# Own buffers for the last rows' queries, a third key load buffer, and six bias groups ahead of the first step

## The chip, the cores and the metric

The kernel runs on one NeuronCore of a Trainium2 chip. The metric is the device time of one execution in microseconds (us). The core has five engines that run side by side, each with its instructions in a fixed order: PE (matrix products and transposes, which it does as matrix products; PEld is its weight load), DVE (vector), ACT (activation functions, copies), POOL (general vector work) and SP, which here only issues DMA transfers. An engine that reaches an instruction whose input is not there yet stands still, and all that is behind it on that engine stands too.

## What is computed

The reference chains three layers on 2 x 576 tokens of width 512: attention with a learnt bias, a token and channel mixer, and a layer of eight experts with one expert chosen for each token. The change touches the first alone:

```python
scores = scale * np.matmul(q, k.transpose(0, 1, 3, 2))          # 2 batches, 8 heads, 576 x 576, head size 64
x = (psi_rel / psi_i)[..., None]                                # log1p(|i - j|) / log1p(max(i, 1))
h = np.maximum(x @ w1 + b1, 0.0)                                # 32 hidden values for each (i, j)
scores = scores + (h @ w2).transpose(2, 0, 1)[None]             # one bias for each head, same in both batches
attn = softmax(scores)                                          # row maximum taken away, exp, divided by the sum
out = np.matmul(attn, v)
```

## The kernel before

**Steps.** Attention runs in 40 steps, each for one pair of heads of one batch and one tile of query rows. The 576 rows are four tiles of 128 and a tail of 64. The tail comes first: steps 0 to 7 (`it == NIT`), eight pairs, four for each batch. Steps 8 to 15 are the first full tile, and so on. In a step `scores` multiplies on PE and calls `softmax_tile`, which adds the bias and finds the row maximum on DVE (L337) and takes exp on ACT (L340); `normalize` (DVE, POOL), `last_T` and `prob_T` (transposes), `values` and `out_T` follow in the same step or the next two.

**Keys.** During the tail every step also transposes the keys of the pair two steps on (`key_T`: PE, copies on ACT and DVE) and splits them in two parts (`key_split`: DVE, L272). Keys are loaded for two pairs at a time by `load_k` (five transfers); `load_k(0)` and `load_k(2)` come in the start, `load_k(4)` too, `load_k(6)` after step 1, and all share two buffers `kn`. `load_v` is ten transfers for one batch.

**Queries.** For tail steps, `tail_split` (POOL) and `tail_T` put the transposed queries into `qts`, two buffers for two steps each. For full steps `query_T`, `query_split` and `query_rest` prepare two steps at a time and write them into the same `qts` with four transfers from SP (`qt<-qs`, 128 KB each, L328). `load_q` reads them from memory into two buffers `qn` (128 KB).

**Bias.** The bias is made in 36 groups of 16 rows. I count them from 0: groups 0 to 3 are the tail's rows, 4 to 11 the first full tile's. For a group, `bias_hidden` makes four 128 x 576 tiles (L487 on ACT, L490 on DVE and POOL), `bias_mm` multiplies them on PE (16 matmuls, L500), ACT copies the result to `ev` (L503), and SP sends `ev` to the rows of the tile `bias` (L509 for the tail, L511 else, 288 KB a group). `ev` has two buffers, so the copy of group n + 2 waits until the transfer of group n has landed. The softmax of a tile needs all its groups. Groups 0 to 4 are made ahead of step 0; then each step makes one (`bias_mm`) and the hidden tiles of the next, so group 11 falls in step 6. Step 7 makes none, and step 8 begins with group 12.

**Order.** Nothing is scheduled by a tool: the lists in `ORDER` say in which order the parts of a step are written down, and each engine takes its share in that order. `start` is what comes ahead of step 0, `first` is for steps 0 to 2, `mixed` for 3 to 7, `bias` for later ones. `load_q` of a step is issued ahead of its list.

Of the kernel before, what the change touches and what calls it, by code (L numbers as in the profile page):

```python
# [9 lines left out]
F32 = mybir.dt.float32  # L10
F32R = mybir.dt.float32r
# [10 lines left out]
B, H, S, D = 2, 8, 576, 64  # L22
# [26 lines left out]
MROWS = E * CAP + 10 * 128  # L49

WARM = 3
AHEAD = 1
QRB = 2
TB = 2
QO = 3, 3, 3, 6

ORDER = {
    "start": "hidden0 const load_k2 tail_split0 hidden1 bias0 hidden2 bias1 key_T00 hidden3 zero key_T01 key_T11 key_T10 key_split0 tail_split1 bias2 hidden4 bias3 load_k4 hidden5 key_split1 tail_T bias4 load_v load_q".split(),
    "first": "scores0 hidden2 last_T prob_T0 values key_T0 normalize query_T tail_T query_split hidden1 hidden0 key_T1 bias_mm key_split out_T tail_split hidden3 query_rest".split(),
    "mixed": "hidden2 scores0 values tail_T query_T normalize hidden0 last_T prob_T0 key_T0 key_T1 query_split tail_split hidden1 key_split query_rest bias_mm out_T hidden3".split(),  # L60
    "bias": "query_T query_split hidden3 scores0 scores1 last_T values hidden0 query_rest hidden2 late bias_mm out_T mix prob_T0 prob_T1 hidden1 normalize".split(),
# [71 lines left out]
def attention(tc, nc, tok, mix, q, k, v, w1, b1, w2, c_L, c_id, ident, x, wt1, wt2, prefill):  # L133
# [4 lines left out]
    NP = H // 2  # L138
# [4 lines left out]
    tw_p = pool(tok, "tokw")  # L143
    with ExitStack() as ctx:
        cst = pool(ctx, "acst")
        bias_p = pool(ctx, "bias", 2)
        nat_p = pool(ctx, "nat")
# [62 lines left out]
        def load_k(i):  # L210

            b, pr = divmod(i, NP)
            n = nat_p.tile([128, 20, D], F32, name="kn", tag="kn", bufs=2)
            main, hs = n[:, 0:16].rearrange("p (n h) d -> p n h d", h=4), k[b, 2 * pr:2 * pr + 4]
            for j in range(NIT):
                nc.sync.dma_start(main[:, j], hs[:, 128 * j:128 * j + 128].rearrange("h p d -> p h d"))
            nc.sync.dma_start(n[0:64, 16:20], hs[:, 512:S].rearrange("h p d -> p h d"))
            for j in range(2):
                nat["k", i + j] = main[:, :, 2 * j:2 * j + 2], n[0:64, 16 + 2 * j:18 + 2 * j]
# [14 lines left out]
        def load_q(it, i):  # L234

            b, pr = divmod(i, NP)
            n = nat_p.tile([128, 4, D], F32, name="qn", tag="qn", bufs=2)
            if it == NIT:
                tv = q[b, :, 512:S].rearrange("(a e) p d -> e p a d", e=2)
                for e in range(2):  # L240
                    nc.sync.dma_start(n[64 * e:64 * e + 64], tv[e])
                for j in range(NP):
                    nat["q", it, i + j] = n[:, j]
            else:
                nc.sync.dma_start(n, q[b, 2 * pr:2 * pr + 4, 128 * it:128 * it + 128].rearrange("h p d -> p h d"))
                nat["q", it, i] = n
# [29 lines left out]
        QT = {}  # L276
        qts = [nat_p.tile([128, 2, 4, 128], F32R, name=f"qt{i}") for i in range(2)]

        def query_tile(s):
            return qts[s // 2 % 2][:, s % 2]  # L280

# [1 line left out]

        def query_zero():

            for qt in qts:
                nc.gpsimd.memset(qt[:, :, 0:2, 64:128].bitcast(F32), 0.0)
                nc.gpsimd.memset(qt[:, :, 2:4, 0:64].bitcast(F32), 0.0)

        def tail_split(it, i):  # L290
            n = nat.pop(("q", it, i))
# [5 lines left out]

        def tail_T(it, i):
            qs = nat.pop(("qs", it, i)).bitcast(F32).rearrange("p a d -> p (a d)")
            QT[it, i] = qt = query_tile(i)  # L300
            tp = alloc_ps()
            for a in range(2):
                nc.tensor.transpose(tp[:, 128 * a:128 * a + 128], qs[:, D * a:D * a + 128], ident)
            tv = tp[:, 0:256].rearrange("p (a i) -> p a i", a=2)
            scaled("qT0", qt[:, 0:2, 0:64], tv[:, :, 0:64])
            scaled("qT1", qt[:, 2:4, 64:128], tv[:, :, 64:128])
# [277 lines left out]
        steps = [(it, i) for it in its for i in range(B * NP)]  # L584
# [23 lines left out]
        def late_fetch(s):  # L608
# [4 lines left out]
        load_const()  # L613
        bias_setup()
        start = {
            "const": (bias_const,), "zero": (query_zero,), "load_k2": (load_k, 2), "load_k4": (load_k, 4), "load_v": (load_v, 0),
            "load_q": (load_q, *steps[NP]), "tail_T": (tail_T, *steps[0]),
        }
        for n in range(2):
# [11 lines left out]
        for s in range(N + 2):  # L631

            bias = gi < len(groups) and s < N and s >= B * NP * (its.index(groups[gi] // 8) - 1)
            at = lambda d, n=N: steps[s + d] if 0 <= s + d < n else None
            two = lambda d: (s + d) % 2 == 0 and s + d >= B * NP and at(d)
            hide = groups[gi + 1] if bias and gi + 1 < len(groups) else None
            todo = {
                "late": (late_step, (s,)), "mix": (mixes[s][0], mixes[s][1:]) if s in mixes else (None, None),
                "tail_split": (tail_split, at(2, B * NP)), "tail_T": (tail_T, at(1, B * NP)),
                "query_T": (query_T, two(QO[0])), "query_split": (query_split, two(QO[1])), "query_rest": (query_rest, two(QO[2])),  # L640
                "key_split": (key_split, at(2, B * NP)),
                "normalize": (normalize, at(0)), "last_T": (last_T, at(-1)),
                "values": (values, at(-2)), "out_T": (out_T, at(-2)),
# [2 lines left out]
            for j in range(4):  # L646
# [1 line left out]
                todo[f"key_T{j}"] = key_T, j < 2 and at(2, B * NP) and (*at(2), j)  # L648
                todo[f"scores{j}"] = scores, at(0) and (*at(0), j)
                todo[f"prob_T{j}"] = prob_T, at(-1) and (*at(-1), j)  # L650
            if two(QO[3]):
                load_q(*steps[s + QO[3]])
            for name in ORDER["edge" if bias and s % (B * NP) == B * NP - 1 else "first" if s < 3 else "mixed" if s < B * NP else "bias" if bias else "plain"]:
                f, a = todo[name]
                if a:
                    f(*(a[1:] if f in (key_split, key_T) else a))
            gi += bias
            late_fetch(s - 1)
            if s == 1:
                load_k(6)  # L660
            if s == 2:
                load_v(1)
            if s == 10:
# [639 lines left out]
class Experts:  # L1303
# [7 lines left out]
    AHEAD = [[f"big{4 * a + c}.0" for c in range(4)] for a in range(2)]  # L1311
# [451 lines left out]
```

## Time and profile before

| | |
|---|---|
| median of 3 runs | 584.0 us (583.43 to 585.43) |
| the profiled execution | 584.03 us, of it the span 582.3 us |
| busy share of the span | PE 94%, DVE 66%, ACT 57%, POOL 42% |
| attention's first 80 us | the tail's steps lie between about 21 and 64 us, step 8 begins at about 64 |

The span is what the profiler saw of the core; all times of rows are counted from its start. A line of a timeline has the start, the duration, the engine, the line of the code, the operation and its tiles, and in brackets how long the engine had been idle and what it waited for last. SPq is SP's queue: the time that the issue of a transfer took, not the transfer. Where a row joins several instructions, "x4" is their number and the duration that of all.

### The profile page before, as it was taken

The page shows a single profiled execution, that of the slowest core. Times are in us where ns is not written, and L with a number is a line of the kernel's source. Part 1 is how long each engine was busy: PE and PEld are TensorE (multiplying, and loading weights), DVE is VectorE, ACT ScalarE, POOL GpSimd, SP SyncE. Part 2 cuts the span into 40 slices and gives each one's busy share as a digit, 9 for nine tenths or more (in the row PEclk, how much of TensorE's full clock was granted, in tenths as well). Part 3 has the DMA queues.
Part 4 walks back from the last instruction along what each step waited for, and adds up shares of the span by engine and source line. Part 5 has one row for each costly group of instructions (what it writes and reads, how often), then busy time and mean ns, then how long its engine had stood idle before and what let it go on. Part 6 is the DMA issues. An engine that isn't in the chain of part 4 may idle for free.

```text
span 582.3 us, 11959 instructions
## 1 busy us (share of the span) xinstructions
PE 545.5 (94%) x4306; PEld 430.3 (74%) x4306; DVE 383.9 (66%) x896; ACT 329.5 (57%) x608; POOL 242.1 (42%) x230
## 2 busy tenths in 40 slices
PE   7689699999899999989999999999999999999992
PEld 3366477777677887869999877787778778787871
DVE  5789588889887675698888535714473235668650
ACT  4678589789898793344444223221423257777760
POOL 4666547476555360044444300310014234657541
PEclk8979889999999999999999999999999999999997
DMA  6997988698697351143443020081002985566950
GB/s 162 130 173 126 142 158 165 132 177 157 127 147 126 77 154 38 37 138 120 148 161 126 1 91 0 1 302 61 19 18 43 370 299 175 147 230 245 367 185 12
DMA packets 72110, 79.90 MB, mean 137 GB/s; under 512 B 36822, under 2 KB 51420, under 8 KB 72044
## 3 DMA queue, kind: packets, MB, share of 16 engines
q1 hardware_dynamic: 67276, 73.72, 50.7%
q0 software_dynamic: 2176, 5.26, 2.7%
q8 instruction: 36, 0.59, 0.5%
q10 hardware_dynamic: 2592, 0.09, 0.3%
q14 instruction: 30, 0.25, 0.2%
HBM read 72.08 MB, written 5.34 MB: 133 GB/s over the span
## 4 chain that ended last, share of the span: by engine, by line
PE 65%; DVE 12%; DMA 7%; issue 5%; ACT 5%; SPq 2%; POOL 2%; ACTq 0%; POOLq 0%; DVEq 0%
PE ph L748 20%; PE po L748 16%; DMA bias<-ev 6%; PE py L748 5%; PE ps L500 5%; PE tp L425 4%; PE ps L359 3%; PE tp L410 3%; DVE t L337 2%; ACT t L340 2%; PE tp L748 1%; DVE K L272 1%; DMA mt<-meta 1%; PE tp L1448 1%; DVE raw L732 1%
## 5 line engine op out<-in xcount | busy, mean ns | idle before, releaser
L490 POOL TENSOR_SCALAR hd<-tabs,sc,negb 128x576 f32<-128x576 f32 x32 | 76.4, 2389 | 4.7 <-PE ps L500 3.0
L340 ACT ACTIVATE t<-t,st 128x576 f32<-128x576 f32 x72 | 55.4, 770 | 28.8 <-DVE st L337 28.4
L748 PE MATMUL po<-cw,h 128*128 128x512 f32 x272 | 67.3, 395 | 0.0
L337 DVE CUSTOM_DVE_ANT_0 t<-ps,bias 128x576 f32<-128x576 f32 x72 | 52.3, 751 | 16.1 <-DMA bias<-ev 6.6
L359 PE MATMUL ps<-K,qt 128*128 128x288 f32 x320 | 54.0, 309 | 4.4 <-DVE qt L199 3.5
L748 PEld LDWEIGHTS po<-cw,h 128*128 128x128 f32 x272 | 49.8, 188 | 10.0 <-issue 0.4
L1411 DVE TENSOR_TENSOR big<-raw,big 128x1024 fp32r<-128x1024 f32 x30 | 42.3, 1433 | 22.4 <-ACT big L1410 22.4
L500 PE MATMUL ps<-hd,wblk 128*32 128x288 f32 x576 | 47.7, 440 | 7.5 <-DVE st L337 6.5
L359 PEld LDWEIGHTS ps<-K,qt 128*128 128x128 f32 x320 | 45.0, 192 | 6.7 <-DVE qt L199 2.3
L425 PE MATMUL tp<-pt,v 128*64 128x128 f32 (+1 forms) x800 | 49.2, 268 | 0.6 <-DVE K L272 0.6
L748 PE MATMUL py<-big,hT 128*128 128x512 f32 x184 | 47.8, 400 | 0.4 <-POOL big L1411 0.4
L1189 POOL DMA_INDIRECT meta<-tokid,posi x10 | 10.0, 996 | 90.7 <-DVE tokid L1186 54.7
L425 PEld LDWEIGHTS tp<-pt,v 128*64 128x64 f32 x800 | 40.1, 137 | 8.1 <-issue 5.1
L1410 ACT CAST big<-raw 128x1024 fp32r<-128x1024 f32 x44 | 44.2, 1055 | 2.8 <-DMA big<-in_moe_w_dram 1.0
L748 PE MATMUL ph<-big,xT 128*128 128x512 f32 x168 | 42.9, 403 | 0.0
L490 DVE TENSOR_SCALAR hd<-tabs,sc,negb 128x576 f32<-128x576 f32 x69 | 42.2, 640 | 1.0 <-PE ps L500 0.9
L748 PEld LDWEIGHTS py<-big,hT 128*128 128x128 f32 x184 | 33.8, 188 | 8.6 <-POOL big L1411 0.9
L740 POOL TENSOR_TENSOR big<-wf,big 128x512 fp32r<-128x512 f32 x12 | 18.8, 1564 | 50.3 <-ACT big L739 50.3
L487 ACT ACTIVATE hd<-tabs,b1c,sc 128x576 f32<-128x576 f32 x43 | 36.9, 866 | 3.8 <-DVE sc L458 3.7
L1411 POOL TENSOR_TENSOR big<-raw,big 128x1024 fp32r<-128x1024 f32 x10 | 27.5, 2747 | 24.9 <-ACT big L1410 24.3
L748 PEld LDWEIGHTS ph<-big,xT 128*128 128x128 f32 x168 | 30.6, 189 | 8.6 <-issue 1.6
L500 PEld LDWEIGHTS ps<-hd,wblk 128*32 128x32 f32 x576 | 17.2, 115 | 24.1 <-DVE st L337 7.9
(302 smaller groups left out, 1204.7 us busy)
## 6 DMA issues: line engine op xcount, KB each, us to landing
raw<-in_moe_w_dram SPq DMA_DIRECT2D x48, 512.0 KB
raw<-in_moe_w_ch_dram SPq DMA_DIRECT2D x24, 512.0 KB
bias<-ev SPq DMA_DIRECT2D x32, 288.0 KB
qt<-qs SPq DMA_DIRECT2D x64, 128.0 KB
lw<-in_moe_w_dram SPq DMA_DIRECT2D x16, 512.0 KB
big<-in_moe_w_dram SPq DMA_DIRECT2D x8, 512.0 KB
lw<-in_moe_w_dram SPq DMA_DIRECT2D x16, 256.0 KB
big<-in_moe_w_dram SPq DMA_DIRECT2D x16, 256.0 KB
```

What stands on the lines that cost most here:

```text
L337: nc.vector.tensor_tensor_reduce(t.rearrange("p (a j) -> p a j", a=2), ps[:, :, 0:HALF], bs.rearrange("p (a j) -> p a j", a=2), op0=ALU.ad ...
L340: nc.scalar.activation(t, t, AF.Exp, bias=st[:, j:j + 1], scale=-1.0, accum_out=st[:, 2 + j:3 + j])
L359: nc.tensor.matmul(ps[:, hf, 0:HALF], lhsT=qt[:, j], rhs=K[k][:, hf * HALF:(hf + 1) * HALF], start=j == pairs[0][0], stop=j == pairs[-1][0])
L410: nc.tensor.transpose(tp[:, 128 * j:128 * j + 128], tt[:, o:o + 128], ident)
L425: nc.tensor.matmul(po[64 * h:64 * h + 64, 0:rhs.shape[1]], lhsT=lhsT, rhs=rhs, start=j == 0, stop=j == 4)
L487: nc.scalar.activation(hd[:, qq], Lt[:, o:o + S], AF.Relu, bias=b1c, scale=sc[:, c])
L490: eng.tensor_scalar(hd[:, qq], Lt[:, o:o + S], sc[:, c], negb, ALU.mult, ALU.max)
L500: nc.tensor.matmul(ps[32 * qq:32 * qq + 32, hf, 0:HALF], lhsT=wblk, rhs=hd[:, qq, hf * HALF:(hf + 1) * HALF], start=True, stop=True)
L740: nc.gpsimd.tensor_tensor(lo, src, hi.bitcast(F32), ALU.subtract)
L748: nc.tensor.matmul(out, lhsT=lhs[a], rhs=rhs[b], start=first and i == 0, stop=last and i == 2)
L1410: nc.scalar.copy(hi, raw)
L1411: (nc.gpsimd if c == 3 and t else nc.vector).tensor_tensor(lo, raw, hi.bitcast(F32), ALU.subtract)
```

## The change

- The tail's queries get a tile of their own, `lastq`, with a place for each of two steps, in memory that `w2s` takes later; `query_zero` clears that in place of `qts`.
- `load_k(4)` goes into a third buffer, `kn2`, in memory that is used later for `wt1_s`. `load_k(6)` thereby takes the first buffer, and is moved from after step 1 to the start, behind `load_v` and `load_q`.
- `AHEAD` is 2: six groups of the bias come ahead of step 0, so hidden tiles of group 6 and the whole of group 5 stand in `start`, group 5 as its last entry. Each group after that is made one step sooner, group 11 in step 5; steps 6 and 7 make none.
- The queries of steps 8 and 9 are prepared in step 4 instead of step 5. All others stay.

```diff
-AHEAD = 1
+AHEAD = 2
-QO = 3, 3, 3, 6
+QO = 3
-    "start": "hidden0 const load_k2 tail_split0 hidden1 bias0 hidden2 bias1 key_T00 hidden3 zero key_T01 key_T11 key_T10 key_split0 tail_split1 bias2 hidden4 bias3 load_k4 hidden5 key_split1 tail_T bias4 load_v load_q".split(),
+    "start": "hidden0 const load_k2 tail_split0 hidden1 bias0 hidden2 bias1 key_T00 hidden3 zero key_T01 key_T11 key_T10 key_split0 tail_split1 bias2 hidden4 bias3 load_k4 hidden5 key_split1 tail_T bias4 load_v hidden6 load_q load_k6 bias5".split(),
...
-            n = nat_p.tile([128, 20, D], F32, name="kn", tag="kn", bufs=2)
+            if i == NP:
+                n = nat_p.tile([128, 20, D], F32, name="kn2", tag="ks")
+            else:
+                n = nat_p.tile([128, 20, D], F32, name="kn", tag="kn", bufs=2)
...
+        lastq = tw_p.tile([128, 2, 4, 128], F32R, name="lastq", tag="w2s")
...
-            for qt in qts:
-                nc.gpsimd.memset(qt[:, :, 0:2, 64:128].bitcast(F32), 0.0)
-                nc.gpsimd.memset(qt[:, :, 2:4, 0:64].bitcast(F32), 0.0)
+            for qt in (lastq[:, 0], lastq[:, 1]):
+                nc.gpsimd.memset(qt[:, 0:2, 64:128].bitcast(F32), 0.0)
+                nc.gpsimd.memset(qt[:, 2:4, 0:64].bitcast(F32), 0.0)
...
-            QT[it, i] = qt = query_tile(i)
+            QT[it, i] = qt = lastq[:, i % 2]
...
-            two = lambda d: (s + d) % 2 == 0 and s + d >= B * NP and at(d)
+            ready = steps[B * NP] if s == B * NP - 4 else s + QO > B * NP and (s + QO) % 2 == 0 and at(QO)
...
-            if two(QO[3]):
-                load_q(*steps[s + QO[3]])
+            if s % 2 == 0 and s + 6 >= B * NP and at(6):
+                load_q(*at(6))
...
-            if s == 1:
-                load_k(6)
```

What that does to the engines' order is shown at three places. The lines of the code are 3 to 5 higher in the changed kernel (L511 is L516, L503 is L508, L340 is L345). What stands in brackets is what the instruction waits for: DMAHW0 to DMAHW7 are eight semaphores that the transfers take in turn.

SP, from the last transfers of `load_v(0)` on, before (`bias` transfers are groups 5, 6 and, in the last row, 7):

```order
L231 DMA v_323<-in_v_dram 64x4x64 [waits DMAHW1_49]
L241 DMA qn<-in_q_dram 64x4x64 [waits DMAHW2_49]
L241 DMA qn<-in_q_dram 64x4x64 [waits DMAHW3_49]
L511 DMA bias_310<-ev 16x8x576 [waits DMAHW4_49,Activation_49]
L511 DMA bias_310<-ev 16x8x576 [waits DMAHW5_49,Activation_49]
L216 DMA kn<-in_k_dram 128x4x64 [waits DMAHW6_49,PE_49]
L216 DMA kn<-in_k_dram 128x4x64 [waits DMAHW7_49]
L216 DMA kn<-in_k_dram 128x4x64 [waits DMAHW0_49]
L216 DMA kn<-in_k_dram 128x4x64 [waits DMAHW1_49]
L217 DMA kn<-in_k_dram 64x4x64 [waits DMAHW2_49]
L245 DMA qn<-in_q_dram 128x4x64 [waits DMAHW3_49,Pool_49]
L511 DMA bias_310<-ev 16x8x576 [waits DMAHW4_49,Activation_49]
```

The same place after (the three `bias` rows are groups 5, 6 and 7):

```order
L234 DMA v_324<-in_v_dram 64x4x64 [waits DMAHW1_49]
L244 DMA qn<-in_q_dram 64x4x64 [waits DMAHW2_49]
L244 DMA qn<-in_q_dram 64x4x64 [waits DMAHW3_49]
L219 DMA kn<-in_k_dram 128x4x64 [waits DMAHW4_49,PE_49]
L219 DMA kn<-in_k_dram 128x4x64 [waits DMAHW5_49]
L219 DMA kn<-in_k_dram 128x4x64 [waits DMAHW6_49]
L219 DMA kn<-in_k_dram 128x4x64 [waits DMAHW7_49]
L220 DMA kn<-in_k_dram 64x4x64 [waits DMAHW0_49]
L516 DMA bias_311<-ev 16x8x576 [waits DMAHW1_49,Activation_49]
L516 DMA bias_311<-ev 16x8x576 [waits DMAHW2_49,Activation_49]
L516 DMA bias_311<-ev 16x8x576 [waits DMAHW3_49,Activation_49]
```

The five key loads have moved ahead of group 5's transfer, and the transfers of groups 5 and 6 behind them.

ACT in step 1, before: exp, a copy of transposed probabilities, two key copies, a hidden tile, the copy to `ev` (group 6), a hidden tile, and the exp of step 2:

```order
L340 ACTIVATE t_399,st_400<-t_399,st_400 128x576 [waits DVE_49]
L193 COPY pt_416<-tp_424 128x5x64 [waits PE_49]
L193 CAST K30_431<-tp_433 64x512 [waits PE_49]
L193 CAST K31_432<-tp_433 64x512
L487 ACTIVATE hd_414<-tabs_99,b1c_101,sc_107 128x576 [waits Activation_49,Pool_49]
L503 ACTIVATE ev_463<-ps_454,cb1_155 128x576 [waits DMAHW7_49,PE_49,Activation_49]
L487 ACTIVATE hd_414<-tabs_99,b1c_101,sc_107 128x576
L340 ACTIVATE t_482,st_483<-t_482,st_483 128x576 [waits DVE_49]
```

The same step after, where the copy to `ev` is group 7's:

```order
L345 ACTIVATE t_423,st_424<-t_423,st_424 128x576 [waits DVE_49]
L193 COPY pt_440<-tp_448 128x5x64 [waits PE_49]
L193 CAST K30_455<-tp_457 64x512 [waits PE_49]
L193 CAST K31_456<-tp_457 64x512
L492 ACTIVATE hd_438<-tabs_99,b1c_101,sc_108 128x576 [waits Activation_49,Pool_49]
L508 ACTIVATE ev_487<-ps_478,cb1_156 128x576 [waits DMAHW1_49,PE_49,Activation_49]
L492 ACTIVATE hd_438<-tabs_99,b1c_101,sc_108 128x576
L345 ACTIVATE t_500,st_501<-t_500,st_501 128x576 [waits DVE_49]
```

The places are the same, but the copy to `ev` waited for semaphore DMAHW7, which is group 4's transfer, and now waits for DMAHW1, which is the first of SP's `bias` rows above, group 5's.

SP in steps 3 to 6, before (bias rows: groups 8, 9, 10 and 11; the `qt` rows are the queries of steps 8 and 9; the first `qn` row loads those of 10 and 11):

```order
L511 DMA bias_310<-ev 16x8x576 [waits DMAHW7_49,Activation_49]
L245 DMA qn<-in_q_dram 128x4x64 [waits DMAHW0_49,Pool_49]
L511 DMA bias_310<-ev 16x8x576 [waits DMAHW1_49,Activation_49]
L328 DMA qt_104<-qs 64x2x256 [waits DVE_49,DMAHW2_49,PE_49,Pool_49]
L328 DMA qt_104<-qs 64x2x256 [waits DMAHW3_49]
L328 DMA qt_104<-qs 64x2x256 [waits DMAHW4_49,DVE_49,PE_49]
L328 DMA qt_104<-qs 64x2x256 [waits DMAHW5_49]
L511 DMA bias_310<-ev 16x8x576 [waits DMAHW6_49,Activation_49]
L245 DMA qn<-in_q_dram 128x4x64 [waits DMAHW7_49,PE_49]
L511 DMA bias_310<-ev 16x8x576 [waits DMAHW0_49,Activation_49]
```

The same place after (bias rows: groups 9, 10 and 11):

```order
L516 DMA bias_311<-ev 16x8x576 [waits DMAHW0_49,Activation_49]
L248 DMA qn<-in_q_dram 128x4x64 [waits DMAHW1_49,Pool_49]
L333 DMA qt_104<-qs 64x2x256 [waits DMAHW2_49,Activation_49]
L333 DMA qt_104<-qs 64x2x256 [waits DMAHW3_49]
L333 DMA qt_104<-qs 64x2x256 [waits DMAHW4_49]
L333 DMA qt_104<-qs 64x2x256 [waits DMAHW5_49]
L516 DMA bias_311<-ev 16x8x576 [waits DMAHW6_49,Activation_49]
L516 DMA bias_311<-ev 16x8x576 [waits DMAHW7_49,Activation_49]
L248 DMA qn<-in_q_dram 128x4x64 [waits DMAHW0_49,PE_49]
```

Group 9 now goes ahead of the query load that waits for POOL, the two last groups directly behind the `qt` rows; the `qt` rows have lost their waits for PE and DVE.

## Rows read from the trace of the kernel before

**Rows 1.** Page, costliest groups: count | busy us, mean ns | idle before.

```profile
L500 PE MATMUL ps<-hd,wblk 128*32 128x288 f32 x576 | 47.7, 440 | 7.5 <-DVE st L337 6.5
...
L487 ACT ACTIVATE hd<-tabs,b1c,sc 128x576 f32<-128x576 f32 x43 | 36.9, 866 | 3.8 <-DVE sc L458 3.7
```

**Rows 2.** Busy time by stretch: length, each engine, granted clock, DMA share, GB/s.

```profile
20.00:24.40 4.40, 2.77 (x27) 2.33 (x31) 1.39 (x4) 1.74 (x3) 2.88 (x5) 1.00 1.10 134
...
36.90:56.50 19.60, 17.24 (x215) 12.28 (x215) 18.45 (x59) 16.24 (x31) 13.39 (x22) 1.00 1.01 147
...
66.90:71.70 4.80, 1.32 (x26) 1.05 (x25) 0.00 (x0) 0.08 (x1) 3.59 (x4) 0.74 1.15 147
```

**Rows 3.** Chain that ended last, 13 to 72 us: start, duration, what.

```profile
13.46 4.91 DMA bias<-ev
...
37.93 0.16 DVE st L370
...
53.35 0.76 DVE t L337
...
57.65 5.64 DMA bias<-ev
...
64.14 7.37 DMA bias<-ev
```

**Rows 4.** Timeline of SP's queue, 20 to 65 us.

```profile
20.52 2.25 SPq L216 DMA_DIRECT2D kn<-in_k_dram  x4
22.82 0.90 SPq L217 DMA_DIRECT2D kn<-in_k_dram  x1
23.82 0.56 SPq L511 DMA_DIRECT2D bias<-ev  x1
...
33.11 1.27 SPq L241 DMA_DIRECT2D qn<-in_q_dram  x2
34.48 1.28 SPq L511 DMA_DIRECT2D bias<-ev  x2
35.85 3.96 SPq L216 DMA_DIRECT2D kn<-in_k_dram  x4
39.85 1.47 SPq L217 DMA_DIRECT2D kn<-in_k_dram  x1
...
57.17 0.38 SPq L245 DMA_DIRECT2D qn<-in_q_dram  x1
57.65 1.66 SPq L511 DMA_DIRECT2D bias<-ev  x1
59.48 2.66 SPq L328 DMA_DIRECT2D qt<-qs  x4
...
64.14 0.58 SPq L511 DMA_DIRECT2D bias<-ev  x1
```

**Rows 5.** Timeline of ACT, copies to `ev` (L503) and exp (L340).

```profile
22.18 0.74 ACT L503 ACTIVATE ev<-ps,cb 128x576 f32<-128x576 f32 x1 [0.39 <-DMA bias<-ev]
...
25.24 0.78 ACT L340 ACTIVATE t<-t,st 128x576 f32<-128x576 f32 x1 [2.31 <-DVE st L337]
...
34.40 0.74 ACT L503 ACTIVATE ev<-ps,cb 128x576 f32<-128x576 f32 x1 [0.39 <-ACT hd L487]
...
36.88 0.78 ACT L340 ACTIVATE t<-t,st 128x576 f32<-128x576 f32 x1 [0.98 <-DVE st L337]
...
63.37 0.74 ACT L503 ACTIVATE ev<-ps,cb 128x576 f32<-128x576 f32 x1 [1.18 <-DMA bias<-ev]
```

**Rows 6.** Timeline of DVE and POOL: softmax of steps 0, 8; last tail query; keys.

```profile
24.44 0.76 DVE L337 CUSTOM_DVE_ANT_0 t<-ps,bias 128x576 f32<-128x576 f32 x1 [2.96 <-PE tp L262]
...
56.82 0.32 POOL L295 TENSOR_TENSOR qm<-qn,qm 128x64 fp32r<-128x64 f32 x1
...
57.20 1.90 DVE L272 TENSOR_TENSOR K<-tp,K 64x512 fp32r<-64x512 f32 x4 [0.52 <-ACT K L193]
...
71.73 0.76 DVE L337 CUSTOM_DVE_ANT_0 t<-ps,bias 128x576 f32<-128x576 f32 x1 [4.87 <-DMA bias<-ev]
```

More of the change, by code (lines that the diff above doesn't have):

```diff
@@ L615, in attention @@
         start = {
-            "const": (bias_const,), "zero": (query_zero,), "load_k2": (load_k, 2), "load_k4": (load_k, 4), "load_v": (load_v, 0),
+            "const": (bias_const,), "zero": (query_zero,), "load_k2": (load_k, 2), "load_k4": (load_k, 4), "load_k6": (load_k, 6), "load_v": (load_v, 0),
             "load_q": (load_q, *steps[NP]), "tail_T": (tail_T, *steps[0]),
@@ L639, in attention @@
                 "tail_split": (tail_split, at(2, B * NP)), "tail_T": (tail_T, at(1, B * NP)),
-                "query_T": (query_T, two(QO[0])), "query_split": (query_split, two(QO[1])), "query_rest": (query_rest, two(QO[2])),
+                "query_T": (query_T, ready), "query_split": (query_split, ready), "query_rest": (query_rest, ready),
                 "key_split": (key_split, at(2, B * NP)),
```

## The prediction

> **What bounds the kernel now.** I read the chain of waits first, then the timelines of the engines that it runs through. As far as step 8 the chain shows two kinds of stretches. From about 38 to 53 us it consists of DVE's own instructions, one behind the other, from the sum's reciprocal of step 2 to the softmax of step 5 [rows 3]; in the stretch that holds these steps DVE is busy 18.45 of 19.6 us [rows 2]. So DVE bounds the tail's middle steps, and what delays DVE there moves all that follows, save for at most 1.15 us of gaps. Then two bias transfers stand on the chain, 5.64 and 7.37 us from the start of the issue to the landing [rows 3]. They are groups 9 and 11. Group 9 was issued at 57.65, right behind a query load that SP could only issue at 57.17 [rows 4], since it waited for POOL to read the last tail query out of the same buffer (56.82 + 0.32 = 57.14) [rows 6]. The copy of group 11 to `ev` waited 1.18 us for group 9's landing [rows 5]. Its own transfer went out at 64.14 [rows 4] and landed 7.37 us on, at 71.5, and the softmax of step 8 began at 71.73, DVE having stood 4.87 us [rows 6]. In that stretch DVE and ACT do nothing, while the DMA engines are busy throughout [rows 2]. So the start of step 8 is set by the landing of group 11, and I ask of each edit what it does to that.
>
> **The third key buffer and the early load.** `load_k(4)` went out in the trace from 20.52 to 23.72 [rows 4], directly behind the bias transfers in the queue, so its buffer cost it no wait: a buffer of its own gives nothing there. `load_k(6)` starts at 34.4, when the query load ends (33.11 + 1.27), instead of 35.85 [rows 4]. Its keys are wanted in step 4 only, so 1.45 us gained there are worth nothing. But its five issues now stand ahead of group 5's transfer. They take 3.2 us, as those of `load_k(4)` do, or up to 5.5, as they did behind two bias transfers (35.85 to 41.32) [rows 4]. The first is nearer, for now too nothing but loads is ahead. So group 5 goes out at 37.6 (latest 39.9), instead of 34.48.
>
> **The sixth group ahead.** Its work fits in the start: from 20.0 to 24.4 us PE idles 1.6 us, DVE 3.0, ACT 2.7 and POOL 1.5 [rows 2], and the first softmax waits until 24.44 [rows 6]. PE needs 47.7 / 36 = 1.3 us for group 5, ACT two hidden tiles and a copy, 2 x 0.87 + 0.74 = 2.5 us [rows 1, 5]. The scores of step 0 now want the accumulator that ACT's copy of group 4 frees at 22.92 [rows 5], and end about when that softmax starts. At most 0.2 us is lost, and the wait below covers that. What comes off in step 6, a matmul block, a copy and hidden tiles, lies ahead of a wait for DMA and is worth nothing while that wait stands.
>
> The cost is the wait for `ev`. In step 1 ACT copies group 7, no longer group 6, and needs the landing of group 5. ACT reached that copy at 34.40 [rows 5]. When does group 5 land? Issue to landing took 4.91 us for a group with a key load just ahead of it, 5.64 and 7.37 for others [rows 3]: 37.6 + 4.9 = 42.5. From the other side, 864 KB (the key load and the group) from 34.4 on at the 147 GB/s of that stretch [rows 2] take 6.0 us: 40.4, without what the queue still held then. The latest is 39.9 + 7.4 = 47.3. I take 41.8, between the first two. Behind the copy ACT has a hidden tile and then the exp of step 2: 41.8 + 0.74 + 0.87 + 0.1 = 43.5, against 36.88 [rows 1, 5]. **ACT stands some 7 us, and the exp of step 2 comes 6.6 us late** (5.2 to 12). DVE's next instruction, the sum's reciprocal at 37.93 [rows 3], wants that exp, with keys, hidden tiles and the later softmaxes queued behind it. PE's bias matmuls of step 2 want the accumulator of group 7 and stand too. The gaps of DVE could take back 1.15 us at most, and since they are the distances between dependent instructions, I take back none.
>
> The Trainium skill (DMA: Bandwidth & Descriptors, section on the anatomy of one DMA) gives a transfer about 2.0 us and its bytes at 436 GB/s, though fitted on another issue path. For 288 KB that is an estimate of 2.7 us. The rows' 4.9 to 7.4 us [rows 3] speak against it here, since transfers queue. By it the landing would be at 40.3 and, worked on as below, the time an estimated 585.2 us, which belongs to the rival of no change.
>
> **Own query buffers and earlier queries.** The waits of the `qt` transfers for PE and DVE go. In the trace they followed the bias transfer by 0.17 us [rows 4], so those waits cost next to nothing. Preparing the queries in step 4 puts two ACT instructions ahead of that step's key copies. In step 5, where they stood, DVE waited 0.52 us for such a copy [rows 6]. Now this comes ahead of the last tail query, so that is late by D = 6.6 + 0.5 = 7.1 us. The query load of step 4 still waits for that query, and the four `qt` transfers, group 10 and group 11 all stand behind it in SP's queue. The smaller clearing of `lastq` on POOL is worth nothing.
>
> **The sum.** Before, from the end of group 9's issue (59.31) to the landing of group 11 (71.51), 12.2 us, the queue moved group 9, four `qt`, group 10, a query load and group 11: 288 + 512 + 288 + 128 + 288 = 1504 KB [rows 3, 4]. After, group 9 is out ahead of the waiting load, and from 57.2 + D on the queue moves 128 + 512 + 288 + 288 = 1216 KB, at the same rate 9.9 us. Group 11 then lands at 57.2 + 9.9 + D = 67.1 + D: without the wait for `ev` 4.4 us sooner, and with D = 7.1 at 74.2, **2.7 us later**. What follows step 8 is the same code, in the same order, and moves with it. The profiled execution was 584.03 us, as good as the median of the runs, 584.0: 584.0 + 2.7 = **586.7 us**. Group 5's landing at 40.4 and no 0.5 give D = 5.2, +0.8 and 584.8; D = 9.2, two us more, gives +4.8 and 588.8.
>
> **Rivals.** *The wait is short or made up (faster).* D up to 2.6 gives a gain of over 0.3%. If the copy of group 7 met a landed group 5, D would be about 0, group 11 would land at 67.1, and the time would be 584.0 - 4.4 = 579.6. For it: what the edits plainly do to SP's later queue, where group 11 no longer waits for group 9. Against it: group 5's transfer would have to land by 37 us, and before 37.6 it isn't even issued; or steps 2 to 5 would have to give back 4.5 us, and DVE has gaps of 1.15 there [rows 2]. *Half and half (no change).* D between 2.6 and 6.1; the transfer lands within some 3 us of its issue, or some of the delay is given back. The break-even is D = 4.4. The time is 582.3 to 585.7. Against it are the durations of bias transfers in [rows 3]. That the edits don't do what they are for, the buffers freeing nothing, ends here too. *The queue is worse (slower still).* With the latest landing, 47.3, D is 12.6 and the time 584.0 + 8.2 = 592.2. It would need the key load to be held up as it was behind two bias transfers [rows 4], which are no longer ahead.
>
> **How the numbers follow.** About 0.3% is what a measurement of this kernel can tell from no change: 582.25 to 585.75. I give the forecast, with its own range from 584.8 to 588.8, 0.55; of that some 0.07 lies within 0.3%. No change by half and half has 0.17, faster 0.20, and worse than 588.8 has 0.08. So slower is 0.48 + 0.08 = 0.56, same 0.07 + 0.17 = 0.24, faster 0.20. Leaving out the 0.08 above and some 0.12 of the faster cases below gives 581.5 to 588.8.
>
> **What would show it.** In the changed kernel's timeline ACT should stand some 7 us ahead of the second copy to `ev` after the first exp (step 1), released by a bias transfer at about 41.8; the exp of step 2 should start near 43.5, and DVE and PE have a hole from about 38 to 44. The query load ahead of the `qt` transfers should go out at about 64.3, groups 10 and 11 right behind these, and the softmax of step 8 start near 74.4 after a wait for DMA shorter than 4.87 us. If ACT doesn't stand at that copy, the forecast is wrong by the whole of D. If step 8 starts late but the end doesn't move, something later was waiting anyway.

## The result, and the profile after

| | before | after |
|---|---|---|
| median of 6 runs each, side by side | 583.71 us (582.31 to 585.53) | 589.63 us (588.44 to 592.68) |
| ratio, 95% interval | | 1.0112 (1.0093 to 1.0130) |
| profiled execution | 584.03 us | 589.45 us |
| its span | 582.3 us | 587.6 us |

The changed kernel is slower by 1.1%, some 6.5 us by the ratio. The forecast was 586.7 us, slower, with a range up to 588.8: the sign and ACT's wait came true, the size was about half of what came (2.7 us of 5.9 by the medians), and the time lies 0.8 us outside the range. The two profiled executions differ by 5.4 us, and the trace can say where these come from.

I read the difference off one operation that occurs in every step, DVE's softmax sum (L337 before, L342 after). After minus before, its first instruction starts at these distances:

| step | 0 to 2 | 3 | 4 | 5 | 6 | 7 | 8 | 10 | from 12 on |
|---|---|---|---|---|---|---|---|---|---|
| us | -0.3 to -0.2 | +7.74 | +7.74 | +8.20 | +7.68 | +7.47 | +4.11 | +5.75 | 5.6 to 5.7 |

So nearly all of it happens in three places: a loss of 7.9 us between steps 2 and 3, a gain of 3.4 ahead of step 8, a loss of 1.6 between steps 8 and 10. From there to the end (+5.3) both kernels run nearly alike.

**The first loss.** ACT's timeline of the kernel after (start, duration, what; in brackets the idle time before it and what ended it):

```profile
42.59 0.74 ACT L508 ACTIVATE ev<-ps,cb 128x576 f32<-128x576 f32 x1 [8.40 <-DMA bias<-ev]
43.23 0.86 ACT L492 ACTIVATE hd<-tabs,b1c,sc 128x576 f32<-128x576 f32 x1
43.99 0.76 ACT L345 ACTIVATE t<-t,st 128x576 f32<-128x576 f32 x1
```

ACT stands 8.40 us for group 5's transfer, and the exp of step 2 behind that copy starts at 43.99, 7.1 us later than in [rows 5]. DVE stands for that exp, and then once more:

```profile
44.88 0.15 DVE L375 TENSOR_SCALAR st<-st 128x1 f32<-128x1 f32 x1 [6.87 <-ACT t L345]
...
49.90 0.76 DVE L342 CUSTOM_DVE_ANT_0 t<-ps,bias 128x576 f32<-128x576 f32 x1 [0.81 <-PE ps L364]
...
59.30 1.90 DVE L275 TENSOR_TENSOR K<-tp,K 64x512 fp32r<-64x512 f32 x4 [0.49 <-ACT K L193]
```

The first row is the start of the reciprocal of [rows 3], 6.95 us later. The second is the softmax of step 3, which waits 0.81 us for PE's scores. The chain that ended last tells why (start, duration, what):

```profile
23.70 5.85 DMA bias<-ev
...
36.99 0.61 SPq L220
37.70 4.79 DMA bias<-ev
...
45.58 2.08 PE ps L505 x16
...
48.06 1.69 PE ps L364 x8
...
58.26 1.11 PE ps L505 x16
```

The first row is group 4's transfer. Group 5's goes out when the key load's fifth issue (L220) is done, and lands after 4.79 us. The bias block of step 2, PE's first after the hole, takes 2.08 us, a later one of the same 16 matmuls 1.11. The engines' busy time by stretch shows the clock under it (length, then busy time and instructions of PE, weight load, DVE, ACT and POOL, then the granted clock, the DMA share and GB/s):

```profile
34.00:36.00 2.00, 0.83 (x10) 0.62 (x8) 1.89 (x5) 0.19 (x1) 2.00 (x4) 0.92 0.37 80
36.00:38.00 2.00, 2.00 (x25) 1.87 (x25) 1.60 (x5) 0.00 (x0) 0.52 (x1) 0.50 0.94 212
37.00:44.00 7.00, 1.82 (x14) 1.30 (x10) 0.61 (x3) 1.41 (x3) 0.00 (x0) 0.50 0.85 142
45.00:49.00 4.00, 3.79 (x23) 2.19 (x24) 3.77 (x11) 3.52 (x7) 3.26 (x6) 0.50 0.71 86
36.90:56.50 19.60, 13.12 (x133) 9.08 (x129) 10.98 (x35) 11.12 (x20) 8.55 (x14) 0.68 0.91 138
```

From 37 to 44 us PE is busy 1.82 of 7 us and has half its clock, 1.2 of 2.4 GHz. The clock did not fall in this hole: it was at half from 36 us on, while PE was still at work, and PE came out of the hole with it and kept it to 49. DVE, busy 18.45 of 19.6 us in this stretch before [rows 2], is busy 10.98.

**The gain ahead of step 8.** SP's queue after:

```profile
65.37 0.38 SPq L248 DMA_DIRECT2D qn<-in_q_dram  x1
65.85 2.60 SPq L333 DMA_DIRECT2D qt<-qs  x4
68.56 1.26 SPq L516 DMA_DIRECT2D bias<-ev  x2
69.91 0.55 SPq L248 DMA_DIRECT2D qn<-in_q_dram  x1
```

The query load starts 8.2 us later than in [rows 4], but groups 10 and 11 now follow the `qt` transfers at once. Group 11 is out at 69.8, against 64.7 before, and the softmax of step 8 comes 4.11 us late, no longer 8.2:

```profile
75.84 0.76 DVE L342 CUSTOM_DVE_ANT_0 t<-ps,bias 128x576 f32<-128x576 f32 x1 [2.63 <-DMA qn<-in_q_dram]
...
81.66 0.76 DVE L342 CUSTOM_DVE_ANT_0 t<-ps,bias 128x576 f32<-128x576 f32 x1 [1.72 <-PE ps L364]
```

The releaser that the first row names is the query load issued right behind group 11 in the same queue; the softmax reads the bias, not the queries. Group 11's own semaphore is full at 75.67 in this trace, the query load's only at 76.01, after the softmax has begun.

**The second loss.** The second row is step 9's softmax (+4.66): it waits 1.72 us for PE, where before it waited 1.09:

```profile
76.99 0.76 DVE L337 CUSTOM_DVE_ANT_0 t<-ps,bias 128x576 f32<-128x576 f32 x1 [1.09 <-PE ps L359]
```

Step 10's comes another 1.1 us late. Busy time by stretch of the kernel before:

```profile
68.00:72.00 4.00, 0.24 (x10) 0.10 (x4) 0.27 (x1) 0.00 (x0) 2.58 (x2) 0.65 1.08 152
72.00:76.00 4.00, 3.45 (x23) 1.63 (x24) 3.76 (x12) 2.45 (x6) 0.00 (x0) 0.50 0.32 74
76.00:80.00 4.00, 4.00 (x54) 3.06 (x54) 2.93 (x9) 3.96 (x9) 2.52 (x2) 0.99 0.83 145
```

And of the kernel after, 4 us later:

```profile
72.00:76.00 4.00, 2.43 (x34) 1.99 (x33) 1.27 (x5) 1.33 (x3) 3.38 (x4) 1.00 0.91 91
76.00:80.00 4.00, 3.34 (x23) 1.52 (x24) 3.38 (x11) 2.37 (x5) 0.92 (x1) 0.58 0.65 148
80.00:84.00 4.00, 4.00 (x37) 3.46 (x41) 1.89 (x6) 3.94 (x8) 1.77 (x2) 0.57 0.86 150
```

Before, PE stood for over 4 us, its clock fell while it stood, and it was back at 2.4 GHz by 76, some 3.5 us after the work began. After, PE stands only about 2 us and still has its full clock when it stands (1.00 up to 76); the half clock begins with the work and lasts to nearly 84. Here the shorter wait costs more: nearly all of the time at 1.2 GHz now falls on the work of steps 8 to 10.

### The profile page after: what moved, and what is told of

Read it like the earlier page. It is cut to its first block, busy times and chain, and to the rows that moved or that the text cites. A ratio compares the mean times of both kernels' runs of the same rounds, so it can differ in the third digit from the quotient of the medians.

```text
span 587.6 us, 11959 instructions
## 1 busy us (share of the span) xinstructions
PE 546.2 (93%) x4306; PEld 431.9 (74%) x4306; DVE 385.8 (66%) x895; ACT 330.1 (56%) x609; POOL 244.7 (42%) x230
## 4 chain that ended last, share of the span: by engine, by line
PE 68%; DVE 9%; DMA 7%; ACT 6%; issue 5%; SPq 2%; POOL 1%; ACTq 0%; POOLq 0%; DVEq 0%
PE ph L751 21%; PE po L751 15%; PE py L751 6%; DMA bias<-ev 6%; PE ps L505 5%; PE tp L430 4%; PE ps L364 4%; PE tp L415 3%; ACT t L345 2%; DVE t L342 2%; PE tp L751 1%; PE tp L1451 1%; SPq L219 1%; PE tp L446 1%; DMA qn<-in_q_dram 1%
## 5 line engine op out<-in xcount | busy, mean ns | idle before, releaser
L345 ACT ACTIVATE t<-t,st 128x576 f32<-128x576 f32 x72 | 55.4, 770 | 24.4 <-DVE st L342 23.9
L342 DVE CUSTOM_DVE_ANT_0 t<-ps,bias 128x576 f32<-128x576 f32 x72 | 52.3, 750 | 15.8 <-PE ps L364 4.9
L505 PE MATMUL ps<-hd,wblk 128*32 128x288 f32 x576 | 45.9, 427 | 7.9 <-DVE st L342 4.4
L364 PE MATMUL ps<-K,qt 128*128 128x288 f32 x256 | 43.9, 313 | 0.0
L492 ACT ACTIVATE hd<-tabs,b1c,sc 128x576 f32<-128x576 f32 x44 | 37.7, 865 | 3.8 <-DVE sc L463 3.7
L508 ACT ACTIVATE ev<-ps,cb 128x576 f32<-128x576 f32 x36 | 26.6, 739 | 23.0 <-DMA bias<-ev 12.2
L364 PEld LDWEIGHTS ps<-K,qt 128*128 128x128 f32 x256 | 36.4, 194 | 0.1
L1414 POOL TENSOR_TENSOR big<-raw,big 128x1024 fp32r<-128x1024 f32 x10 | 26.3, 2628 | 20.4 <-ACT big L1413 20.4
```

What stands on the lines that cost most here:

```text
L342: nc.vector.tensor_tensor_reduce(t.rearrange("p (a j) -> p a j", a=2), ps[:, :, 0:HALF], bs.rearrange("p (a j) -> p a j", a=2), op0=ALU.ad ...
L345: nc.scalar.activation(t, t, AF.Exp, bias=st[:, j:j + 1], scale=-1.0, accum_out=st[:, 2 + j:3 + j])
L364: nc.tensor.matmul(ps[:, hf, 0:HALF], lhsT=qt[:, j], rhs=K[k][:, hf * HALF:(hf + 1) * HALF], start=j == pairs[0][0], stop=j == pairs[-1][0])
L492: nc.scalar.activation(hd[:, qq], Lt[:, o:o + S], AF.Relu, bias=b1c, scale=sc[:, c])
L505: nc.tensor.matmul(ps[32 * qq:32 * qq + 32, hf, 0:HALF], lhsT=wblk, rhs=hd[:, qq, hf * HALF:(hf + 1) * HALF], start=True, stop=True)
L508: nc.scalar.activation(ev.rearrange("p (a b) -> p a b", a=2), ps[:, :, 0:HALF], AF.Identity, bias=cbs[hidden_by(g).replace("P", "V")])
```

## The experiments

The theory: ACT's copies go to two `ev` buffers in turn, so a copy waits for the transfer two groups back; a group's transfer that stands late in SP's queue holds ACT, with exp, DVE and PE behind it. The rival: what costs is something else in the change (the query work moved to step 4, the sixth group in the start, the buffers). Each time is a median beside runs of the kernel before on the same chip (583.6, 583.7 and 583.3 us in the three batches); "step 8" is the start of its softmax, and its distance from the 71.73 us of [rows 6].

**A third `ev` buffer in the kernel after** (`ev3`).

```
- ev = nat_p.tile([128, S], F32, name="ev", bufs=2)
+ ev = nat_p.tile([128, S], F32, name="ev", bufs=3)
```

> The changed kernel with three buffers for the bias copies `ev` instead of two; nothing else. Theory A (the loss is ACT's stand at the copy of group 7, which waits for group 5's transfer behind the early key load): with a third buffer that copy needs only group 4's landing at about 29.6, so ACT does not stand; the 8.4 us wait goes to 0, the softmax of step 8 starts about 8 us sooner than 75.8, at 67 to 68, and the time is about 581 us, some 3 us under the kernel before. Rival B (the early key load itself, or the query load that holds back the four query transfers in SP's queue, costs the time whatever ACT does): step 8 stays later than 73 and the time is 586 to 590.

581.45 us, 0.9965 (0.9949 to 0.9982). ACT's timeline of `ev3`, the copies of groups 7 and 8:

```profile
32.94 0.74 ACT L508 ACTIVATE ev<-ps,cb 128x576 f32<-128x576 f32 x1
...
41.11 0.74 ACT L508 ACTIVATE ev<-ps,cb 128x576 f32<-128x576 f32 x1 [2.42 <-PE tp L308]
```

DVE's timeline of it, step 8's softmax:

```profile
67.81 0.76 DVE L342 CUSTOM_DVE_ANT_0 t<-ps,bias 128x576 f32<-128x576 f32 x1 [2.80 <-DMA qn<-in_q_dram]
```

The wait in step 1 is gone, and with it 8.2 us: one buffer takes the kernel from 589.6 to 581.5, with every edit of the change in place. But ACT still stands 2.42 us, in step 2, which the expectation had at 0. The row names PE, yet all that the copy needs of PE, group 8's bias block, ends at 38.0; with three buffers it also needs group 5's transfer, which goes out at 36.26 and whose semaphore is full at 41.03:

```profile
36.26 1.94 SPq L516 DMA_DIRECT2D bias<-ev  x3
36.83 1.18 PE L505 MATMUL ps<-hd,wblk 128*32 128x288 f32 x16
```

It is the same wait, one step later and shorter. Step 8 starts 3.92 us earlier than in the kernel before, close to the 4.4 that the prediction gave for its sum without the wait.

**The place of group 5's transfer.** If the queue is the cause, moving the one transfer must do it too, with two buffers. Four kernels, `swap`, `early5`, `early5_late6` and `ahead1`, move it or what stands around it. `swap` puts it ahead of the early key load:

```
- ... load_v hidden6 load_q load_k6 bias5
+ ... load_v hidden6 load_q bias5 load_k6
```

> The changed kernel with the early key load behind the bias of group 5 in the start instead of ahead of it. Theory A: group 5's transfer goes out at 34.2 and lands at about 39.1, so ACT stands some 4.5 us in step 1 instead of 8.4, step 8 starts 3.5 us sooner, near 72.3, and the time is about 586 us. Rival B (the place of the key load is indifferent): 589 to 590.

585.71 us, 1.0041 (1.0025 to 1.0057), step 8 at 72.92. The transfer goes out at 35.3 instead of 37.7, and the stand of 8.40 us shrinks by more than that. ACT's timeline:

```profile
40.12 0.74 ACT L508 ACTIVATE ev<-ps,cb 128x576 f32<-128x576 f32 x1 [5.10 <-DMA bias<-ev]
```

`early5` puts the whole group, and so its transfer, right behind group 4, ahead of values, queries and keys:

```
- ... tail_T bias4 load_v hidden6 load_q load_k6 bias5
+ ... tail_T bias4 bias5 load_v hidden6 load_q load_k6
```

> The changed kernel with the bias of group 5 directly behind that of group 4 in the start, ahead of the value and key loads; two `ev` buffers, early key load as in the changed kernel. Theory A (only the place of group 5's transfer in SP's queue matters to the copy of step 1): it goes out at about 24.9 and lands by 32, so ACT does not stand in step 1; the next copy that waits is group 8's in step 2, for group 6, which is now the one behind the key load and lands at 42.4, so ACT stands some 2.3 us there instead of 8.4; step 8 starts at about 70 and the time is 582.5 to 584. Rival B (place of the transfer is indifferent): 588 to 590.

584.55 us, 1.0008 (0.9981 to 1.0034), step 8 at 71.52: 5 us better than the kernel after, and somewhat short of what was expected. ACT no longer stands in step 1; now group 6's transfer is behind the key load, and the wait has moved to step 2 of ACT's timeline, 3.72 us instead of the 2.3 expected:

```profile
45.06 0.74 ACT L508 ACTIVATE ev<-ps,cb 128x576 f32<-128x576 f32 x1 [3.72 <-DMA bias<-ev]
```

`early5_late6` also puts the key load back where it was, behind step 1 (in the loop `if s == 1: load_k(6)`).

> As the run before (group 5's bias ahead of the value load), with the last key load put back behind step 1. Theory A: no bias transfer of groups 5 and 6 stands behind the key load, ACT waits less than 1 us in steps 1 and 2, step 8 starts near 68, and the time is 581 to 582, as with three buffers. Rival B: 584 or more.

582.40 us, 0.9991 (0.9976 to 1.0006), between theory A's range and rival B's. The largest such wait left in ACT's timeline of steps 1 and 2 is this one,

```profile
41.57 0.74 ACT L508 ACTIVATE ev<-ps,cb 128x576 f32<-128x576 f32 x1 [0.25 <-DMA bias<-ev]
```

and step 8 comes at 69.19, 2.54 us earlier than in the kernel before. Own query buffers, the third key buffer and six groups ahead are all still there. So the loss at step 8 is the place of two rows in SP's queue, and the rest of the change does bring step 8 forward; the time of the whole kernel isn't told apart from the kernel before.

`ahead1` leaves the early key load and takes back the sixth group (`AHEAD = 1`, start list `load_v load_q load_k6`).

> The changed kernel with five groups ahead as before; own query buffers, third key buffer and the early key load stay. Theory A: group 5 is then copied in step 0 but its transfer still goes out behind the key load at 37.7 and lands at 42.5; the copy that waits is now group 7's in step 2, reached at 40.1, so ACT stands only 2.4 us. Group 9 goes out behind the four query transfers, group 11 waits for it as in the kernel before, so step 8 starts at 73 to 74.5 and the time is 585.5 to 587. Rival C (all of the loss is the sixth group's): 584 or less.

586.10 us, 1.0042 (1.0026 to 1.0058). ACT stands in step 2, as expected, but for longer than the 2.4 us I had written. Its timeline:

```profile
45.47 0.74 ACT L508 ACTIVATE ev<-ps,cb 128x576 f32<-128x576 f32 x1 [5.41 <-DMA bias<-ev]
```

The profiled execution (590.55 us) was above this kernel's median; in it the transfer took 8.22 us from issue to landing, and step 8 starts at 76.21, not at 73 to 74.5. The median is as expected.

**Each part alone, on the kernel before.** `only_ahead2` has the sixth group alone, `k6only` the third key buffer and the early key load, `ownq` the own query buffers with the queries in step 4.

> The kernel before with six bias groups ahead alone: old query buffers, two key buffers, the last key load after step 1. Theory A: group 5 goes out at about 34.2 and lands at 39, the copy of group 7 in step 1 still waits for it some 4.5 us, so the tail runs 4 to 5 us late; the transfers behind it gain 4 (group 11 no longer waits for group 9), so step 8 starts at about 72 and the time is 584 to 585. Rival C (the sixth group ahead is good in itself, the other two parts spoil it): 580 to 581.

584.59 us, 1.0021 (1.0003 to 1.0038), step 8 at 73.20. ACT stands 5.65 us in step 1 of its timeline:

```profile
39.85 0.74 ACT L503 ACTIVATE ev<-ps,cb 128x576 f32<-128x576 f32 x1 [5.65 <-DMA bias<-ev]
```

> The kernel before with the third key buffer and the early key load alone. Theory A: group 5's transfer goes out behind that load at 37.2 instead of 34.5; the copy of group 7 in step 2, reached at 40.1, waits 2 to 5 us for its landing; the tail runs that much late and the bias transfers of groups 9 to 11 with it, so step 8 starts 2 to 5 us later than 71.7 and the time is 585.5 to 588. Rival C (the key load costs nothing without the sixth group): 583 to 584.5.

586.13 us, 1.0045 (1.0029 to 1.0062), step 8 2.1 us late. ACT's timeline, the copy of group 7 in step 2:

```profile
43.80 0.74 ACT L506 ACTIVATE ev<-ps,cb 128x576 f32<-128x576 f32 x1 [3.09 <-PE tp L390]
```

The row names PE, but the chain that ended last goes through a bias transfer that lands at 38.26 + 5.46 = 43.72, just ahead of the copy:

```profile
38.26 5.46 DMA bias<-ev
```

> The kernel before with the queries' part of the change alone: own buffers for the last rows' queries and the queries of steps 8 and 9 prepared in step 4. Theory A: no copy to `ev` waits longer in steps 0 to 3; the query transfers go out at about 57.7, but group 9 now stands behind them, so group 11's copy waits for it as before and step 8 starts at 71.7 to 73: 584 to 585. Rival C (the queries' part brings the time by itself): under 582.

584.69 us, 1.0020 (0.9999 to 1.0040), step 8 0.7 us late. Here group 9 stands behind the query load and the `qt` transfers, and the copy of group 11 waits for it in ACT's timeline:

```profile
66.82 0.74 ACT L505 ACTIVATE ev<-ps,cb 128x576 f32<-128x576 f32 x1 [4.58 <-DMA bias<-ev]
```

None of the three is faster alone, and two are slower. The rival falls: where ACT waits, it waits for a transfer back to `ev` in all of them, in another step each time. Their losses add up to some 5 us (0.0021 + 0.0045 + 0.0020 of 584), near the loss of all together; since the waits are not the same, that is no sum of parts.

**A third `ev` buffer in the kernel before** (`before_ev3`), to see how much of `ev3`'s time belongs to the buffer.

> The kernel before with three `ev` buffers, nothing else. Theory A (in the kernel before only group 11's copy waits for a buffer, 1.18 us; the gain of the changed kernel with three buffers comes from the change's own edits, once ACT does not stand): group 11 goes out some 1 us sooner, step 8 starts at 70.5 to 71.7, the time is 582.5 to 584. Rival D (the third buffer alone makes that gain): 580.5 to 582.

581.91 us, 0.9983 (0.9962 to 1.0003): the rival's figure, though no change lies within the interval. Already step 0 starts 1.4 us earlier, since the copies of groups 2 to 4 wait less (0.5 us in all instead of 1.7), and step 8 starts 1.63 us earlier in DVE's timeline:

```profile
70.10 0.76 DVE L337 CUSTOM_DVE_ANT_0 t<-ps,bias 128x576 f32<-128x576 f32 x1 [5.78 <-DMA bias<-ev]
```

Step 8 gains 2.3 us more from the change's edits (3.92 in `ev3`), but the medians, 581.45 and 581.91, aren't told apart. So with three buffers the change is worth little at the end. Why is the next experiment's matter.

**PE's clock behind step 8** (`warm`, `ev3_warm`). Three matmuls of 128x128 by 128x512 into an accumulator that nobody reads stand in PE's order ahead of step 8's bias block. They change what PE does while the bias is awaited; besides, they take one turn of the ring of four small accumulators.

```
+ if s == 8 and name == "bias_mm":
+     wps = alloc_ps()
+     for _ in range(3):
+         nc.tensor.matmul(wps, lhsT=ident, rhs=Lt[:, 0:512], start=True, stop=True)
```

> The changed kernel with three products of 128 x 128 by 128 x 512 on PE ahead of the bias block of step 8, whose result nobody reads. In the changed kernel PE idles from about 74.4 to 76.6 us, its clock is granted at half from then to 83, and between steps 8 and 10 the kernel falls another 1.6 us behind the kernel before. Theory A (that 1.6 us is PE at the lower of its two levels): with the gap filled the clock stays at the upper level, steps 8 to 10 take 1.6 to 2.5 us less, the time is 587 to 588 us. Rival (the 1.6 us has another cause, or the added products only delay the bias block by their own 0.9 us each): 589.5 to 591.

588.06 us, 1.0091 (1.0056 to 1.0126), the profiled span 585.1 us, 2.5 shorter than the kernel after's. Busy time by stretch of `warm`:

```profile
76.00:80.00 4.00, 4.00 (x30) 1.81 (x29) 3.44 (x11) 2.50 (x6) 1.51 (x1) 1.00 0.56 129
80.00:84.00 4.00, 4.00 (x55) 3.05 (x54) 3.21 (x10) 3.97 (x8) 1.94 (x2) 1.00 0.89 150
```

The clock stays at 1.00 where the kernel after had 0.58 and 0.57, and from step 8 to step 10 the distance goes from +4.69 to +4.24 instead of from +4.11 to +5.75. The interval of the whole time overlaps the kernel after's, so these 2 us rest on the steps of the trace, not on the medians. Of the 2.5 us of the span, 1.2 are there from step 11 on (+4.37 against +5.57). Another 1.2 come only at steps 24 and 25, where the clock is at 1.00 in both kernels; they are not the clock's, and their cause is not shown.

> The changed kernel with three `ev` buffers and the three unread products on PE ahead of the bias block of step 8. Theory A (two separate costs of the change: ACT's stand, and PE at half clock behind step 8): both are gone, so the offset against the kernel before stays at -3.9 us from step 8 on or grows to -5, and the time is 579 to 580 us, under every other run. Rival: the added products cost what the clock gives, 581 to 582.

579.51 us, 0.9941 (0.9918 to 0.9964), the lowest median of all: 0.6% faster than the kernel before, 1.7% faster than the one after. With the third buffer alone PE had half its clock behind step 8, by the stretch of `ev3`:

```profile
68.00:72.00 4.00, 3.37 (x23) 1.55 (x24) 3.35 (x11) 2.37 (x5) 0.71 (x1) 0.50 0.63 144
```

Now it has all of it, by the same stretch of `ev3_warm`:

```profile
68.00:72.00 4.00, 4.00 (x31) 1.89 (x30) 3.54 (x11) 2.72 (x7) 1.28 (x1) 1.00 0.59 136
```

In `ev3` the 3.92 us of step 8 were 3.16 at step 10 and about 2.8 later; in `ev3_warm` 3.50 at step 8 became 3.98 at step 10. So of the 2.3 us that the change's edits had gained at step 8 in `ev3`, 1.1 went back to the clock. It did not all last in `ev3_warm` either: its softmax of step 16 waits 2.85 us where that of `ev3` waits 0.98, which leaves 2.0 us there, and 3.1 at step 36. The spans of the two profiled executions differ by 1.0 us, the medians, from two chips, by 1.9; their intervals overlap a little, so how much the products give beyond step 10 is not settled.

**The query load later** (`ev3_late`), a miss. In `ev3` step 8 still waits 2.80 us for the bias, with a query load and four `qt` transfers ahead of it. I moved the load behind step 5, out of their way.

```
- if s % 2 == 0 and s + 6 >= B * NP and at(6):
+ if s % 2 == 0 and s != 4 and s + 6 >= B * NP and at(6):
+ (after the step's work)  if s == 5: load_q(*at(5))
```

> The changed kernel with three `ev` buffers, and with the query load of step 4 moved behind step 5, so that nothing in SP's queue waits for the last tail query ahead of the four query transfers. Theory A (with ACT's stand gone, the start of step 8 is set by the landing of group 11, which stands behind that load): the query transfers go out at about 55 and group 11 at about 60 instead of 61, lands near 65, step 8 starts when the engines are through with step 7, at about 66 instead of 67.8, and the time is about 579.5 us, 2 under the run with three buffers alone. Rival (the load's place is indifferent, the transfers are bound by the DMA engines): 581 to 582.

582.60 us, 0.9999 (0.9977 to 1.0021), step 8 at 69.67, not 66. The bias is there in time, but PE's timeline has a new wait:

```profile
66.62 0.66 PE L319 MATMUL tp<-ident,qn 128*128 128x128 f32 x2 [3.35 <-DMA qn<-in_q_dram]
```

The load went out at 59.57, and the wait ended 6.92 us later. PE transposes these queries (L319) ahead of step 8's scores, and stands for them 3.35 us; the scores come late, and DVE's softmax with them. I had moved a transfer and not looked for its next reader.

## Why the prediction was right in kind and short in size

The wait was forecast rightly; the step that failed is the one that let all behind a wait move as a block ("what follows step 8 ... moves with it", and no term for PE in D). The traces show PE's clock in its place: 0.8 us ahead of step 3 and 1.6 us behind step 8, most of the 3.0 us that were missed.

- **Where ACT stands, and why: right.** The issue of group 5 came at 37.70 (forecast 37.6), ACT stood 8.40 us at the copy named ("some 7"), and the hole of DVE and PE runs from about 38 to 45 us. `ev3` and `early5` show that this wait, not the rest of the change, makes the loss.
- **The landing of group 5: 0.8 us short, and the 42.5 near by luck.** The landing came 4.79 us after the issue. The prediction took a row of 4.91 [rows 3] for "a group with a key load just ahead", which gives 42.5, and then 41.8, between that and a bound from the throughput that left out what the queue still held. The copy started at 42.59. But the row of 4.91 is no group's: it is the fourth of the tail's eight transfers, of half a group each, and three of these stand between it and the key load. In the queue and the list of transfers of the kernel before:

```profile
11.48 8.94 SPq L509 DMA_DIRECT2D bias<-ev  x8
...
bias<-ev SPq DMA_DIRECT2D x8, 144.0 KB
```

  The transfer that is like it, group 4's of 288 KB with a key load just ahead, took 5.85 us in the kernel after. That 42.5 was so near is luck; whole groups took 4.8 to 8.2 us. The Trainium skill (DMA: Bandwidth & Descriptors, section on the anatomy of one DMA, a fit for another issue path) would have an estimated 2.7 us there; the trace disagrees, with 4.79.
- **PE at half clock in the tail: a term left out.** The prediction let every step behind the wait move as a block. But PE's clock had fallen to 0.50 by 36 us, ahead of the hole, and was still there when PE began again at 45 (2.08 us for the bias block, against 1.11), and DVE waited 0.81 us for the scores of step 3. That this wait is the clock's is read off these durations; no run kept the clock up there. The Trainium skill (TensorE: Matmul & The Clock Gate, section "Loop structure matters more than you think") says that a long wait for DMA between matmuls lets PE run on at the low clock; the kernel before agrees behind its own long wait (1.00 until 69, 0.50 from 72 to 76 us), while of the hole in the tail the trace shows only that the clock stayed low.
- **The queries in step 4: right.** DVE's wait for a key copy was 0.49 us (forecast 0.5), and step 5 is at +8.20 where step 4 was at +7.74.
- **D, the delay at the last tail query: 8.2 us, forecast 7.1.** POOL read that query at 65.02, against 56.82 in [rows 6]. The exp of step 2 came 7.1 us late, 0.5 more than forecast: the landing was 0.8 later, but copy, hidden tile and exp followed each other in 1.4 us instead of 1.7. PE added 0.8, and 0.2 of it all was made up by DVE: so the missing 1.1.
- **The queue from there: right but for 0.4 us.** From the query load at 65.37 to step 8's softmax at 75.84 are 10.5 us. The forecast had 64.3 and 74.4, or 10.1. So step 8 came 4.1 us late, not 2.7, nearly all of it D.
- **"What follows step 8 ... moves with it": wrong, +1.6 us.** This is the largest single miss. The wait ahead of step 8 became shorter (DVE's from 4.87 to 2.63 us), as forecast, and I took a shorter wait as harmless. Yet the clock now fell where the work begins, and steps 8 to 10 lost 1.6 us. `warm` keeps the clock up, and the loss doesn't come.
- **What was priced at nothing and was nothing:** the sixth group's own work (steps 0 to 2 even come 0.2 to 0.3 us early) and the smaller clearing on POOL. The early key load isn't among them: its benefit is nothing, as forecast, and `k6only` gives its cost alone, 0.45%.
- **The rivals.** "Short or made up" had 579.6 us if the copy met a landed group; `ev3` comes near this case: POOL read the last tail query at 56.81, so D was 0.0, and step 8 came within 0.5 us of the working. That D was so small is partly the third buffer's doing, since the tail began 1.1 us earlier and lost as much behind ACT's wait in step 2. Its 581.45 are 1.9 us more than the rival's time; the trace shows 1.1 of them behind step 8, at half clock. The "worse queue" had its price on the wrong place: the queue held as forecast, and the time lay outside the range since 0.8 us (PE ahead of step 3) and 1.6 us (steps 8 to 10) had no place in it.

Added up: 2.7 us forecast, 1.4 more at step 8 (1.1 by D, the rest by the queue), 1.6 behind it: 5.7 us from step 10 on, and 5.3 at the end of the span.

Open stays how much of `ev3`'s gain is the change's own and how much the third buffer's, which the medians don't separate. Open is also why some bias transfers of the same 288 KB took 4.8 us and others 8.2 with the same kind of load ahead; the traces show the durations, not what the queue did in them.

## What to carry to other kernels

An engine that copies into a ring of buffers, emptied by transfers on one in-order queue, can stand when that queue is given something to do first: when a load is moved earlier or a producer further ahead, count ring depth against the queue's rows, since the wait is paid by all that is queued behind the copy on that engine. A delay doesn't move the steps behind it as a block: ask at what clock PE goes into the hole and comes out of it, price its first blocks from a row at half clock, and see whether the low clock falls on idle time or on work. Before a row's duration is taken for the case in hand, look up what the row moved: here it was half the bytes.

## What was not expected of the hardware

A hole of about 2 us in PE's work ahead of step 8, at full clock until then, was followed by some 7 us at 0.50; the longer hole of the kernel before was followed by only some 3.5 us of work at that clock. Three unread matmuls in the hole kept the clock at 1.00 and were worth more than they cost.
